# Squared scores read from PSUM, another split of the low parts, and routing candidates written to PSUM

## The chip, the cores and the metric

The kernel runs on one core of one Trainium2 chip. The metric is the device time of one execution in microseconds (us). "The engines" are TensorE (PE in the profile, PEld for its weight loads), VectorE (DVE), ScalarE (ACT), GpSimd (POOL) and SyncE (SP), which issues the DMAs. Each takes its own instructions strictly in the order in which the program lists them, and waits on semaphores of the others.

## What is computed

```python
# u, v: (8, 3136, 256), z: (8, 3136, 64); float32; capacity 128
scores = (1.0 / S) * np.matmul(z, z.transpose(0, 2, 1))
attn = np.maximum(scores, 0.0) ** 2
x = u * np.matmul(attn, v)
s = np.einsum('bsd,d->bs', x, w_gate)
for b in range(B):                       # the 128 tokens of highest s pass through an FFN
    top_idx = np.argpartition(-s[b], capacity)[:capacity]
    xe = x[b, top_idx]
    ye = np.maximum(xe @ w1, 0.0) @ w2
    g = 1.0 / (1.0 + np.exp(-s[b, top_idx]))
    out[b, top_idx] = xe + g[:, None] * ye
```

## The kernel before

**Tiling.** For each of 8 batches the columns of the attention matrix (tokens of the output) are cut into seven chunks: five of 512 and two of 288. The rows come in 24 blocks of 128 and a remainder of 64. A *slot* is one pair of row blocks against one chunk (`slots`, L259): 12 pairs and one single (the remainder) per chunk, 91 slots a batch. The matrix is symmetric, so what lies below the diagonal of whole chunks has been computed before: such an *old* slot fetches its squares from DRAM (`fetch`), a *new* slot computes them. Chunk 0 has new slots alone, chunk 1 has 10 new pairs and 2 old, chunk 2 has 8 and 4, and chunks 5 and 6 have 2 and 10.

**Precision.** Every float32 operand is split in a rounded high part and the low remainder. A new slot takes four score matmuls (`sc`, L314: two row blocks, two halves of Z), an old one none; each pair slot takes 12 matmuls into the two accumulators (`acc`, L391): eight with the high part `hi` of the squares, four with the low part `lo`.

**A new slot's way.** PE writes the scores to `sc` (PSUM; two buffers of two banks each). ACT makes `a` = relu(scale x `sc`) (L317, two buffers) and `hi` = round(`a` squared) (L319). Then `a` is squared in place, by DVE as `a` times `a` (L324) or, when the planner's counters hold DVE for busier than ACT, by ACT (L322). In `low`, DVE transposes `a` in two pieces for the symmetric half (`aT`, L341; SyncE stores it), and `lo` = `a` - `hi` is made by POOL or DVE (L352). `low` of an old slot does only the last step, from `qk`.

**Order.** The program is written out by hand, slot by slot (L1045 on). `mix(k)` emits the 12 accumulation matmuls of slot k and, in the middle of them, the scores of slot k+3; behind it stand the routing steps due in that slot and `low` of slot k+3. A table `busy` of estimated work per engine (`spend`) picks the engine for the squares and for `lo`. At a chunk's end `finish` multiplies both accumulators with `u` on DVE (`ut`, L436), which frees them; there are three accumulator banks, and a chunk takes two.

**Routing.** The 128 best tokens of a batch are found during the next batch, as a search for the threshold in eight rounds of four bits. A round is: PE adds up counts over partitions (`tot`, L556); DVE settles the four bits (`enough`, `mi`, `base`, L561 to L567), makes 15 candidates out of a table of keys in three operations on 98 partitions x 15 numbers (`cand`, `flip`, `key`, L533, L524, L528), compares all scores with them (`ge`, L542) and counts (`cnt`, L550). Rounds stand three slots apart (two in the last batch), so they fall into chunks 0, 1 and 2 of the next batch. The last batch, which has nobody behind it, routes most of its tokens during its own chunks.

Of the kernel before, what the change touches and what calls it, by code (L numbers as in the profile page):

```python
# [10 lines left out]
F32 = mybir.dt.float32  # L11
# [7 lines left out]
P = 128  # L19
# [58 lines left out]
def attention_then_routed_ffn(ctx: ExitStack, tc: tile.TileContext, zt, ut, v, wg, w1, w2, cst, cst16, keys, outs, at, cap):  # L78
# [158 lines left out]
    def prep_v(b, g):  # L237
# [11 lines left out]
        spend(act=0.6, pool=1.5)  # L249
# [53 lines left out]

    def scores(k):
# [12 lines left out]
        nc.scalar.activation(a, ps[:, :n], AF.Relu, scale=SCALE)  # L317
        rows = slice(0, P) if n == 2 else slice(64, P)
        nc.scalar.activation(hi, a, AF.Square)  # L319
        on_act = n == 2 and busy["dve"] > busy["act"]  # L320
        if on_act:
            nc.scalar.activation(a, a, AF.Square)  # L322
        else:
            nc.vector.tensor_tensor(a[rows], a[rows], a[rows], op=ALU.mult)  # L324
        of = w * n
        act, dve = 0.15 + 0.00083 * of, 0.1 + 0.0011 * of
        spend(act=(3 if on_act else 2) * act, dve=0.0 if on_act else dve)
        lows.append((k, a, hi, None))

    def low(k, a, hi, by):  # L330
# [15 lines left out]
        if n == 2:  # L346
            lo = work.tile([P, 2, CH], F32R, name="lo", tag="lo", bufs=LEAD)[:, :, :w]
            on, took = nc.vector, 0.1 + 0.0026 * w
            if busy["pool"] + 0.8 + 0.0034 * w < busy["dve"] + took:
                on, took = nc.gpsimd, 0.65 + 0.0034 * w  # L350
# [3 lines left out]
        else:  # L354
            nc.vector.tensor_tensor(hi[rows], a[rows], hi[rows].bitcast(F32), op=ALU.subtract)
            spend(dve=0.1 + 0.0013 * w)
# [72 lines left out]
    def finish(b, c):  # L429
# [5 lines left out]
        for h in range(NK):  # L435
            nc.vector.tensor_tensor(xT[:, h, :w], acc[b, c][h], xT[:, h, :w], op=ALU.mult)  # L436
        spend(dve=0.1 + 0.0026 * w)
# [6 lines left out]
        def turn(h):  # L444
# [8 lines left out]
            if scored:  # L453
# [6 lines left out]
                spend(pool=0.65 + 0.0034 * w)  # L460
# [40 lines left out]
    def route(b):  # L501
# [18 lines left out]
        def to_float(k):  # L520

            n = k.shape[1]
            m = moe.tile([TP, n], I32, name="flip", tag=f"flip{n}")[:R]
            nc.vector.tensor_scalar(  # L524
                m, k, 31, 0x7FFFFFFF, op0=ALU.arith_shift_right, op1=ALU.bitwise_and
            )
            f = moe.tile([TP, n], I32, name="key", tag=f"key{n}")[:R]
            nc.vector.tensor_tensor(f, k, m, op=ALU.bitwise_xor)  # L528
            return f.bitcast(F32)

        def tries(rd):
            k = moe.tile([TP, NS], I32, name="cand", tag="cand")[:R]
            nc.vector.tensor_scalar(  # L533
                k, consts["keys"][:R, rd * NS : (rd + 1) * NS], st["base"], None, op0=ALU.bitwise_xor
            )
            st["f"] = to_float(k)
            spend(dve=0.6)

        def count():
# [12 lines left out]
            spend(dve=1.3)  # L552
# [5 lines left out]
        def settle(rd):  # L558
# [570 lines left out]
```

## Time and profile before

| what | value |
|---|---|
| runs | median 2385.51 us of 3 (2382.0 to 2386.51) |
| the profiled execution | 2383.7 us, span 2381.9 us |
| PE busy | 2177.3 us (91% of the span) |
| DVE busy | 1866.6 us (78%) |
| ACT busy | 1283.3 us (54%) |
| POOL busy | 1218.1 us (51%) |
| DMA queue of SyncE | 397.66 MB, 67.5% of 16 engines' span |
| granted TensorE clock | 0.970 |

The span runs from the first to the last instruction. Busy time counts an engine's instructions, also while one of them stands and waits inside for something that it shares with another engine; time between instructions is idle time, and the profile names what ended it. Where a row gives `min/median/max`, these are durations in ns of one instruction of that kind. Batches 1 to 6 repeat nearly exactly; batch 0 has a start and no routing beside it, batch 7 has the late routing and the end.

### The profile page before, as it was taken

What the parts mean: (1) busy time and instruction counts of PE and PEld (TensorE: products, weight loads), DVE (VectorE), ACT (ScalarE), POOL (GpSimd) and SP (SyncE); (2) the same over time, 40 slices, a digit from 0 to 9 for tenths busy, and PEclk for the clock granted to TensorE, in tenths of its full rate; (3) what the DMA queues carried; (4) which work ended last, traced back from release to release, by engine and by line L of the source; (5) the groups of instructions that cost most, each with busy time, mean ns of one, the idle gap of its engine ahead of it and who ended that gap; (6) DMA issues with size and microseconds to landing.
All of it is one profiled execution on the core that took longest, in us unless ns stands there. A gap on an engine that the chain in (4) does not pass through costs nothing. (4 is left out here: it accounts for less than half of the span.)

```text
span 2381.9 us, 30970 instructions
## 1 busy us (share of the span) xinstructions
PE 2177.3 (91%) x10593; PEld 1796.8 (75%) x10593; DVE 1866.6 (78%) x2409; ACT 1283.3 (54%) x1502; POOL 1218.1 (51%) x573
## 2 busy tenths in 40 slices
PE   7999988999889998899988999889998899899887
PEld 4778966789667886678866788668886688777676
DVE  6767688876898778986789767897688877887876
ACT  5665555546555465554655546545474555655432
POOL 5664264543556445554555536465374553645532
PEclk8999999999999999999999999999998999999989
DMA  4798855698457974589745996468964588546762
GB/s 132 186 266 185 178 145 135 165 218 196 142 135 183 212 196 130 144 198 205 190 130 146 203 218 187 118 151 188 231 183 119 156 173 197 161 131 142 166 142 65
DMA packets 505758, 401.73 MB, mean 169 GB/s; under 512 B 125952, under 2 KB 416768, under 8 KB 501888
## 3 DMA queue, kind: packets, MB, share of 16 engines
q1 hardware_dynamic: 504832, 397.66, 67.5%
q0 software_dynamic: 768, 2.10, 0.3%
q8 instruction: 83, 1.36, 0.3%
q14 instruction: 75, 0.61, 0.1%
HBM read 225.07 MB, written 162.00 MB: 163 GB/s over the span
## 5 line engine op out<-in xcount | busy, mean ns | idle before, releaser
L391 PE MATMUL acc<-hi,V 128*128 128x512 f32 (+1 forms) x5376 | 1267.6, 374 | 63.0 <-DVE ut L436 57.0
L391 PEld LDWEIGHTS acc<-hi,V 128*128 128x128 f32 x5376 | 952.8, 192 | 296.1 <-DVE ut L436 70.3
L352 POOL TENSOR_TENSOR lo<-a,hi 128x1024 fp32r<-128x1024 f32 (+1 forms) x276 | 661.8, 2401 | 813.6 <-DVE a L324 365.0
L317 ACT ACTIVATE a<-sc 128x1024 f32<-128x1024 f32 (+3 forms) x408 | 379.6, 931 | 638.8 <-PE sc L314 399.0
L391 PE MATMUL acc<-lo,V 128*128 128x512 f32 (+1 forms) x2688 | 679.2, 369 | 25.8 <-POOL lo L352 20.8
L391 PEld LDWEIGHTS acc<-lo,V 128*128 128x128 f32 x2688 | 481.3, 191 | 126.6 <-POOL lo L352 34.9
L324 DVE TENSOR_TENSOR a<-a 128x1024 f32<-128x1024 f32 (+3 forms) x270 | 380.1, 1408 | 238.7 <-ACT hi L319 228.5
L319 ACT ACTIVATE hi<-a 128x1024 fp32r<-128x1024 f32 (+3 forms) x408 | 394.0, 966 | 80.1 <-PE acc L391 64.4
L352 DVE TENSOR_TENSOR lo<-qk,hi 128x576 fp32r<-128x576 f32 (+1 forms) x257 | 351.8, 1377 | 71.2 <-ACT hi L300 62.9
L341 DVE STREAM_TRANSPOSE aT<-a 128x512 f32<-128x512 f32 (+1 forms) x520 | 338.8, 686 | 73.5 <-ACT a L322 51.2
L300 ACT CAST hi<-qk 128x1024 fp32r<-128x1024 f32 (+1 forms) x320 | 273.5, 860 | 211.6 <-PE acc L391 171.7
L314 PE MATMUL sc<-Z,ZL 128*128 128x512 f32 (+1 forms) x760 | 295.7, 390 | 10.1 <-DVE ZL L114 10.1
L314 PE MATMUL sc<-Z,ZH 128*128 128x512 f32 (+1 forms) x760 | 294.8, 389 | 7.3 <-ACT ZH L113 4.3
L114 POOL TENSOR_TENSOR V<-vst,V 128x512 fp32r<-128x512 f32 x96 | 171.7, 1792 | 69.5 <-ACT V L113 69.4
L454 POOL TENSOR_TENSOR ut<-x,w_run 128x1024 f32<-128x1024 f32 (+1 forms) x52 | 135.2, 2600 | 130.4 <-DVE x L445 119.0
L352 POOL TENSOR_TENSOR lo<-qk,hi 128x1024 fp32r<-128x1024 f32 (+1 forms) x63 | 140.7, 2235 | 73.8 <-ACT hi L300 54.1
L314 PEld LDWEIGHTS sc<-Z,ZL 128*128 128x128 f32 x760 | 145.3, 191 | 43.5 <-DVE ZL L114 11.8
L314 PEld LDWEIGHTS sc<-Z,ZH 128*128 128x128 f32 x760 | 145.1, 191 | 36.3 <-ACT ZH L113 5.2
L322 ACT ACTIVATE a<-a 128x1024 f32<-128x1024 f32 (+1 forms) x138 | 137.0, 993 | 4.4
L352 DVE TENSOR_TENSOR lo<-a,hi 128x1024 fp32r<-128x1024 f32 (+1 forms) x76 | 106.2, 1398 | 27.0 <-ACT a L322 25.5
L533 DVE TENSOR_SCALAR cand<-k_sb,base 98x15 int32<-98x15 int32 (+1 forms) x64 | 103.5, 1617 | 2.2
L114 POOL TENSOR_TENSOR ZL<-zst,ZH 128x512 fp32r<-128x512 f32 (+2 forms) x49 | 72.3, 1476 | 33.1 <-ACT ZH L113 33.1
(131 smaller groups left out, 1150.0 us busy)
## 6 DMA issues: line engine op xcount, KB each, us to landing
squares<-aT SPq DMA_DIRECT2D x240, 512.0 KB
qk<-squares SPq DMA_DIRECT2D x320, 256.0 KB
qk<-squares SPq DMA_DIRECT2D x320, 144.0 KB
vst<-in_v SPq DMA_DIRECT2D x96, 256.0 KB
ut<-in_ut SPq DMA_DIRECT2D x40, 512.0 KB
out<-x SPq DMA_DIRECT2D x160, 128.0 KB
zst<-in_zt SPq DMA_DIRECT2D x72, 128.0 KB
wh<-w1h_there SPq DMA_DIRECT2D x6, 1024.0 KB
```

Of the source, the lines that this page charges most:

```text
L114: (lo_on or nc.vector.tensor_tensor)(lo, src, hi.bitcast(F32), op=ALU.subtract)
L300: nc.scalar.copy(by(hi), src)
L314: nc.tensor.matmul(ps[:, q], z[:, j * P : (j + 1) * P], mov, start=start, stop=not start)
L317: nc.scalar.activation(a, ps[:, :n], AF.Relu, scale=SCALE)
L319: nc.scalar.activation(hi, a, AF.Square)
L322: nc.scalar.activation(a, a, AF.Square)
L324: nc.vector.tensor_tensor(a[rows], a[rows], a[rows], op=ALU.mult)
L341: nc.vector.transpose(to, a[rows, q].rearrange("p (t m a) -> p t m a", t=GT, a=Q))
L352: on.tensor_tensor(by(lo), a, by(hi).bitcast(F32), op=ALU.subtract)
L391: nc.tensor.matmul(ac[h], w, mov, start=first and h not in started, stop=stop)
L454: nc.gpsimd.tensor_tensor(wx, runs, consts["wg_run"].rearrange("p (o r) -> p o r", o=1).broadcast_to([P, NB, RUN]), op=ALU.mult,)
L533: nc.vector.tensor_scalar(k, consts["keys"][:R, rd * NS : (rd + 1) * NS], st["base"], None, op0=ALU.bitwise_xor)
```

## The change

Four things, all of them in `scores`, `low`, `finish` and `route`:

1. `a` = relu(`sc`) without the scale; the square is made as `sc` times `a`, with `sc` read from PSUM by DVE. The scale moves into `finish`, which becomes a `scalar_tensor_tensor`.
2. ACT takes the third square only when it is behind DVE by the planner's counters with that work included.
3. The planner tries POOL first for `lo`, with other costs, and gives it to DVE only when POOL is behind by 1.2 us more.
4. Candidates: the keys of round 0 are flipped on the host, the base is kept flipped from round 0 on, and a round's 15 candidates come from one operation, which writes them into columns 128 to 142 of the PSUM bank that holds the totals; `ge` reads them there.

By kind of instruction: squares of pairs on DVE go from 214 to 303 (207 to 273 of them 1024 wide), on ACT from 138 to 49. `lo` on DVE goes from 333 to 260, on POOL from 339 to 412. Sixty-four `cand`, 64 `flip` and 64 `key` become 56 one-step candidates and 8 copies; three one-number operations a batch move from the last round to the first.

```diff
     keys = [(steps << sh) & 0xFFFFFFFF for sh in range(32 - BITS, -1, -BITS)]
+    keys[0] ^= 1 << 31
+    keys[0] = np.where(keys[0] >> 31, keys[0] ^ 0x7FFFFFFF, keys[0])
...
+        act, dve = 0.13 + 0.0008 * w * n, 0.15 + 0.00104 * w * n
+        turned = 0.16 + 0.00118 * w * n if turns(k) else 0.0
-        nc.scalar.activation(a, ps[:, :n], AF.Relu, scale=SCALE)
+        nc.scalar.activation(a, ps[:, :n], AF.Relu)
         nc.scalar.activation(hi, a, AF.Square)
-        on_act = n == 2 and busy["dve"] > busy["act"]
-        if on_act:
+        if n == 2 and busy["act"] + 3 * act < busy["dve"] + dve + turned:
             nc.scalar.activation(a, a, AF.Square)
         else:
-            nc.vector.tensor_tensor(a[rows], a[rows], a[rows], op=ALU.mult)
+            nc.vector.tensor_tensor(a[rows], ps[rows, :n], a[rows], op=ALU.mult)
...
-            on, took = nc.vector, 0.1 + 0.0026 * w
-            if busy["pool"] + 0.8 + 0.0034 * w < busy["dve"] + took:
-                on, took = nc.gpsimd, 0.65 + 0.0034 * w
+            on, took = nc.gpsimd, 0.1 + 0.0042 * w
+            dve = 0.05 + 0.002 * w
+            if busy["pool"] + took > busy["dve"] + dve + (1.2 if busy["pool"] > 0 else 0.0):
+                on, took = nc.vector, dve
...
-            nc.vector.tensor_tensor(xT[:, h, :w], acc[b, c][h], xT[:, h, :w], op=ALU.mult)
+            nc.vector.scalar_tensor_tensor(
+                xT[:, h, :w], acc[b, c][h], SCALE * SCALE, xT[:, h, :w], op0=ALU.mult, op1=ALU.mult
+            )
...
         def tries(rd):
-            k = moe.tile([TP, NS], I32, name="cand", tag="cand")[:R]
-            nc.vector.tensor_scalar(
-                k, consts["keys"][:R, rd * NS : (rd + 1) * NS], st["base"], None, op0=ALU.bitwise_xor
-            )
-            st["f"] = to_float(k)
+            f = st["ps"][:R, 128 : 128 + NS]
+            k = consts["keys"][:R, rd * NS : (rd + 1) * NS]
+            if rd == 0:
+                nc.vector.tensor_copy(f, k.bitcast(F32))
+            else:
+                nc.vector.tensor_scalar(f.bitcast(I32), k, st["base"], None, op0=ALU.bitwise_xor)
+            st["f"] = f
...
+            if rd == 0:
...
+                nc.vector.tensor_scalar(
+                    k, mi, 32 - BITS, INT_MIN, op0=ALU.logical_shift_left, op1=ALU.bitwise_xor
+                )
...
+                nc.vector.tensor_scalar(
+                    flip, k, 31, 0x7FFFFFFF, op0=ALU.arith_shift_right, op1=ALU.bitwise_and
+                )
+                nc.vector.tensor_tensor(base, k, flip, op=ALU.bitwise_xor)
```

What it moves, at two places. DVE's queue where batch 3 goes from chunk 0 to chunk 1, from the second round's settling up to `finish` (`ut` are the two products that free the accumulators). Before:

```order
L324 TENSOR_TENSOR a<-a 128x1024 x2
L561 TENSOR_SCALAR enough,m<-tot 98x15
L565 CAST mi<-m 98x1
L567 TENSOR_SCALAR base<-mi,base 98x1
L533 TENSOR_SCALAR cand<-k_sb,base 98x15
L524 TENSOR_SCALAR flip<-cand 98x15
L528 TENSOR_TENSOR key<-cand,flip 98x15
L542 TENSOR_TENSOR ge<-G,key 98x480
L550 TENSOR_REDUCE cnt<-ge 98x15
L436 TENSOR_TENSOR ut<-acc,ut 128x512 x2
```

DVE's queue at the same place, as changed (the candidates are now `tot`, in the totals' bank):

```order
L332 TENSOR_TENSOR a<-sc,a 128x1024 x2
L563 TENSOR_SCALAR enough,m<-tot 98x15
L567 CAST mi<-m 98x1
L571 TENSOR_SCALAR place<-mi 98x1
L575 TENSOR_SCALAR flip<-place 98x1
L578 TENSOR_TENSOR base<-place,flip 98x1
L537 TENSOR_SCALAR tot<-k_sb,base 98x15
L544 TENSOR_TENSOR ge<-G,tot 98x480
L552 TENSOR_REDUCE cnt<-ge 98x15
L444 SCALAR_TENSOR_TENSOR ut<-acc,ut 128x512 x2
```

The order is the same; the three 15-wide operations ahead of `ge` are one, and in this one round of a batch the base takes three one-number operations in place of one.

PE's queue early in batch 0, one slot's matmuls with what they wait for (the first score matmul of a slot waits until its PSUM buffer is free). Before:

```order
L391 MATMUL acc<-hi,V 128x512 [waits Activation_49]
L391 MATMUL acc<-hi,V 128x512 x7
L314 MATMUL sc<-Z,ZH 128x512 [waits Activation_49]
L314 MATMUL sc<-Z,ZL 128x512
L314 MATMUL sc<-Z,ZH 128x512
L314 MATMUL sc<-Z,ZL 128x512
L391 MATMUL acc<-lo,V 128x512 [waits Pool_49]
```

PE's queue at the same place, as changed:

```order
L399 MATMUL acc<-hi,V 128x512 [waits Activation_49]
L399 MATMUL acc<-hi,V 128x512 x7
L320 MATMUL sc<-Z,ZH 128x512 [waits DVE_49]
L320 MATMUL sc<-Z,ZL 128x512
L320 MATMUL sc<-Z,ZH 128x512
L320 MATMUL sc<-Z,ZL 128x512
L399 MATMUL acc<-lo,V 128x512 [waits Pool_49]
```

The matmuls stand as they stood; the score buffer is now released by DVE's product in place of ACT's relu.

More of the change, by code (lines that the diff above doesn't have):

```diff
@@ L248, in prep_v @@
             V[b, 2 * g + q] = t[:, :, :, q * P : (q + 1) * P]
-        spend(act=0.6, pool=1.5)
+        spend(act=0.6, pool=1.3)
     slots = []
@@ L302, in old_scores, with turns @@
         lows.append((k, src, hi, by))
+    def turns(k):
+        b, c, js, _ = slots[k]
+        return c < WHOLE and js[0] * P >= CHUNKS[c][0] + CH
     def scores(k):
@@ L316, in scores @@
         hi = work.tile([P, 2, CH], F32R, name="hi", tag="hi2", bufs=LEAD)[:, :n, :w]
-        nc.scalar.activation(a, ps[:, :n], AF.Relu, scale=SCALE)
-        rows = slice(0, P) if n == 2 else slice(64, P)
+        act, dve = 0.13 + 0.0008 * w * n, 0.15 + 0.00104 * w * n
+        turned = 0.16 + 0.00118 * w * n if turns(k) else 0.0
+        nc.scalar.activation(a, ps[:, :n], AF.Relu)
         nc.scalar.activation(hi, a, AF.Square)
-        on_act = n == 2 and busy["dve"] > busy["act"]
-        if on_act:
+        if n == 2 and busy["act"] + 3 * act < busy["dve"] + dve + turned:
             nc.scalar.activation(a, a, AF.Square)
+            spend(act=3 * act)
         else:
[L324 to L327, printed above, removed]
+            rows = slice(0, P) if n == 2 else slice(64, P)
+            nc.vector.tensor_tensor(a[rows], ps[rows, :n], a[rows], op=ALU.mult)
+            spend(act=2 * act, dve=dve)
         lows.append((k, a, hi, None))
@@ L336, in low @@
         rows = slice(0, P) if n == 2 else slice(64, P)
-        if c < WHOLE and js[0] * P >= c0 + w:
+        if turns(k):
             t = work.tile([P, 2, CH], F32, name="aT", tag="aT", bufs=2)
@@ L341, in low @@
                 nc.vector.transpose(to, a[rows, q].rearrange("p (t m a) -> p t m a", t=GT, a=Q))
-                spend(dve=0.1 + 0.0013 * w)
+                spend(dve=0.08 + 0.00118 * w)
             at = js[0] * P - c0 - w
@@ L355, in low @@
             nc.vector.tensor_tensor(hi[rows], a[rows], hi[rows].bitcast(F32), op=ALU.subtract)
-            spend(dve=0.1 + 0.0013 * w)
+            spend(dve=0.05 + 0.001 * w)
         parts[k] = (hi, lo)
@@ L435, in finish @@
         for h in range(NK):
-            nc.vector.tensor_tensor(xT[:, h, :w], acc[b, c][h], xT[:, h, :w], op=ALU.mult)
-        spend(dve=0.1 + 0.0026 * w)
+            nc.vector.scalar_tensor_tensor(
+                xT[:, h, :w], acc[b, c][h], SCALE * SCALE, xT[:, h, :w], op0=ALU.mult, op1=ALU.mult
+            )
+        spend(dve=0.1 + 0.0023 * w)
         del acc[b, c]
@@ L459, in turn @@
                 )
-                spend(pool=0.65 + 0.0034 * w)
+                spend(pool=0.1 + 0.0042 * w)
         def add():
@@ L515, in start @@
             nc.vector.tensor_copy(G, st["ps"][:R, :NT])
-            st["base"] = moe.tile([TP, 1], I32, name="base", tag="base", bufs=2)[:R]
-            nc.vector.memset(st["base"], INT_MIN)
             tries(0)
[L520 to L525, printed above, removed]
-            )
-            f = moe.tile([TP, n], I32, name="key", tag=f"key{n}")[:R]
-            nc.vector.tensor_tensor(f, k, m, op=ALU.bitwise_xor)
-            return f.bitcast(F32)
-        def tries(rd):
-            k = moe.tile([TP, NS], I32, name="cand", tag="cand")[:R]
-            nc.vector.tensor_scalar(
-                k, consts["keys"][:R, rd * NS : (rd + 1) * NS], st["base"], None, op0=ALU.bitwise_xor
-            )
-            st["f"] = to_float(k)
-            spend(dve=0.6)
+        def tries(rd):
+            f = st["ps"][:R, 128 : 128 + NS]
[5 more added lines that the diff above has]
+            st["f"] = f
+            spend(dve=0.2)
         def count():
@@ L551, in count @@
             st["n"] = n
-            spend(dve=1.3)
+            spend(dve=1.4)
         def total():
@@ L566, in settle @@
             base = moe.tile([TP, 1], I32, name="base", tag="base", bufs=2)[:R]
-            nc.vector.tensor_scalar(
-                base, mi, 32 - BITS * (rd + 1), st["base"], op0=ALU.logical_shift_left, op1=ALU.bitwise_xor
-            )
+            if rd == 0:
+                k = moe.tile([TP, 1], I32, name="place", tag="place")[:R]
+                nc.vector.tensor_scalar(
+                    k, mi, 32 - BITS, INT_MIN, op0=ALU.logical_shift_left, op1=ALU.bitwise_xor
+                )
+                flip = moe.tile([TP, 1], I32, name="flip", tag="flip")[:R]
+                nc.vector.tensor_scalar(
+                    flip, k, 31, 0x7FFFFFFF, op0=ALU.arith_shift_right, op1=ALU.bitwise_and
+                )
+                nc.vector.tensor_tensor(base, k, flip, op=ALU.bitwise_xor)
+            else:
+                nc.vector.tensor_scalar(
+                    base, mi, 32 - BITS * (rd + 1), st["base"], op0=ALU.logical_shift_left, op1=ALU.bitwise_xor
+                )
             st["base"] = base
-            spend(dve=0.9)
+            spend(dve=0.6)
         def masks():
-            t = to_float(st["base"])
+            t = st["base"].bitcast(F32)
             mk = moe.tile([TP, 2 * NT], BF16, name="mk", tag="mk")[:R]
```

## The prediction

> **What bounds the kernel now.** I read the page first, then the busy time by stretch, then the waits, then the order of time around the longest wait.
>
> ```profile
> span 2381.9 us, 30970 instructions
> PE 2177.3 (91%) x10593; PEld 1796.8 (75%) x10593; DVE 1866.6 (78%) x2409; ACT 1283.3 (54%) x1502; POOL 1218.1 (51%) x573
> ```
>
> PE leads with 91%, so over the whole span only what PE spends waiting can be won. Where it waits is a question of stage. The next rows are busy time by stretch: chunks 1 and 2 of batch 0, which has no routing beside it, then chunks 0, 1 and 2 of batch 3, beside which batch 2 is routed (each stretch runs from a chunk's first accumulation matmul to the next chunk's).
>
> ```profile
> core 0: us, PE busy (x) PEld busy (x) DVE busy (x) ACT busy (x) POOL busy (x), PEclk, DMA share, GB/s
> 81.90:128.30 46.40, 44.40 (x192) 35.42 (x191) 32.71 (x35) 29.94 (x32) 31.59 (x15) 1.00 0.62 177
> 128.30:170.80 42.50, 40.98 (x179) 33.31 (x178) 28.05 (x31) 27.71 (x30) 29.99 (x14) 1.00 0.91 285
> 876.60:924.50 47.90, 45.46 (x198) 36.55 (x197) 43.78 (x48) 33.13 (x38) 33.57 (x17) 1.00 0.62 180
> 924.50:986.30 61.80, 49.12 (x195) 38.12 (x194) 53.69 (x73) 29.87 (x30) 29.72 (x13) 0.92 0.43 120
> 986.30:1034.20 47.90, 42.72 (x186) 33.59 (x185) 41.62 (x62) 25.62 (x26) 26.31 (x12) 1.00 0.62 151
> ```
>
> Chunk 1 is the same attention work in both batches, yet takes 46.4 us in batch 0 and 61.8 in batch 3. DVE is busy 32.7 us in the one and 53.7 in the other: more than the 46.4 that the chunk would need, so DVE bounds this stretch and PE waits, its granted clock down to 0.92. Chunk 2 shows the same in little (42.5 and 47.9). Now the waits of PE, over the span:
>
> ```profile
> PE acc L391 <- DVE ut L436: 57.0, 19, 6.4
> PE tot L556 <- DVE cnt L550: 56.1, 22, 6.4
> ```
>
> Both are waits for DVE: for the products that free the accumulators, and for a round's counts. The longest at the start of chunk 1 of batch 3, in order of time:
>
> ```profile
> 925.62 2.60 DVE L324 TENSOR_TENSOR a<-a 128x1024 f32<-128x1024 f32 x1 [0.99 <-ACT hi L319]
> ...
> 928.79 1.96 DVE L533 TENSOR_SCALAR cand<-k_sb,base 98x15 int32<-98x15 int32 x1
> 930.78 2.25 DVE L524 TENSOR_SCALAR flip<-cand 98x15 int32<-98x15 int32 x1
> 933.06 0.17 DVE L528 TENSOR_TENSOR key<-cand,flip 98x15 int32<-98x15 int32 x1
> 933.27 0.66 DVE L542 TENSOR_TENSOR ge<-G,key 98x480 bf16<-98x480 f32 x1
> 933.96 0.66 DVE L550 TENSOR_REDUCE cnt<-ge 98x15 bf16<-98x480 bf16 x1
> 934.53 1.28 DVE L436 TENSOR_TENSOR ut<-acc,ut 128x512 f32<-128x512 f32 x2
> ```
>
> POOL's rows at the same time, and PE's:
>
> ```profile
> 928.37 2.35 POOL L352 TENSOR_TENSOR lo<-a,hi 128x1024 fp32r<-128x1024 f32 x1 [1.22 <-DVE enough L561]
> 930.67 2.32 POOL L352 TENSOR_TENSOR lo<-qk,hi 128x1024 fp32r<-128x1024 f32 x1
> ```
>
> ```profile
> 935.27 2.07 PE L391 MATMUL acc<-hi,V 128*128 128x512 f32 x4 [6.40 <-DVE ut L436]
> ```
>
> `cand` works on 15 numbers and takes 1.96 us: it ends at 930.75, just as POOL's 2.35 us end (930.72). `flip` ends at 933.03, as POOL's next does (932.99). `key`, with POOL idle, takes 0.17. So some DVE operations stand still until POOL's running one is over. The durations by line say which:
>
> ```profile
> L324 DVE TENSOR_TENSOR a<-a x270: 455/1226/3350, 12.3 to 2345.5; 128x1024 f32<-128x1024 f32 x111, 64x288 f32<-64x288 f32 x15, 64x512 f32<-64x512 f32 x9
> L533 DVE TENSOR_SCALAR cand<-k_sb,base x64: 225/2005/2457, 335.3 to 2275.5; 98x15 int32<-98x15 int32 x56, 48x15 int32<-48x15 int32 x8
> L436 DVE TENSOR_TENSOR ut<-acc,ut x112: 442/679/684, 84.4 to 2351.9; 128x512 f32<-128x512 f32 x80, 128x288 f32<-128x288 f32 x32
> ```
>
> The product of `a` with itself, both operands in SBUF, reaches 3.35 us against a median of 1.23, and `cand` is nearly always slow; `ut`, with one operand in PSUM, never spreads (684 at most, 679 in the middle), wherever POOL stands.
>
> **The change part by part.** *The square from PSUM.* Its price before is the 1507 ns mean of chunk 1 in the rows below. After, the form is that of `ut`, one operand in PSUM: 442 ns at 288 elements and 679 at 512 is 1.06 ns an element, so 1.22 us at 1024, without spread. No row is a reason for less; the upper end is the 1.51 of today, if reading `sc` were to block as well. I take 1.22, `ut` being the same form. The Trainium skill, Trace Analysis, "Optimizing Scalar/DVE Operations", speaks against this edit: it gives DVE some 60 ns of access overhead on SBUF and 125 on PSUM. By that a product would cost 65 ns more, an estimate of 23 us of DVE time over 359 products. The trace does not show it: `ut` from PSUM takes 679 ns where the 64x512 product from SBUF takes 0.69 us (the row at 921.36 below).
>
> *Candidates.* The groups of DVE in chunk 1 of batch 3 (count, then busy us and mean ns):
>
> ```profile
> L324 DVE TENSOR_TENSOR a<-a 128x1024 f32<-128x1024 f32 (+1 forms) x7 | 10.5, 1507 | 3.3 <-ACT hi L319 3.2
> L533 DVE TENSOR_SCALAR cand<-k_sb,base 98x15 int32<-98x15 int32 x5 | 7.4, 1486 | 0.2
> L524 DVE TENSOR_SCALAR flip<-cand 98x15 int32<-98x15 int32 x4 | 7.1, 1763 | 0.1
> L528 DVE TENSOR_TENSOR key<-cand,flip 98x15 int32<-98x15 int32 x4 | 5.0, 1242 | 0.1
> L542 DVE TENSOR_TENSOR ge<-G,key 98x480 bf16<-98x480 f32 x4 | 4.4, 1096 | 0.0
> ```
>
> Three operations, 7.4 + 7.1 + 5.0 = 19.5 us, become five of a kind that no row shows (SBUF to PSUM). Nearest are the unblocked `key` and `cand` (0.17 us, and 225 ns at the least); the far end is `cand` as it is, 1.5 us. I take 0.22, by `cand` without POOL: 1.1 us. `ge` has one operand in PSUM then, and I take it as unblocked too, 4 x 0.66 = 2.6 for 4.4 (at worst no gain). The three one-number steps that move into round 0 stood in the last round; no sum.
>
> *The planner.* In chunk 1 the squares on DVE go from 6 pairs to 8, `lo` on DVE from 2 to 1. Squares: 8 x 1.22 + 0.69 = 10.4 for 10.5. `lo`: 1.2 less.
>
> DVE in chunk 1: 53.7 - 19.5 + 1.1 - 1.8 - 0.1 - 1.2 = 32.2 us. That is what batch 0 has there (32.7), in 46.4 us. So chunk 1 stops being bound by DVE, and I price it by batch 0's row, plus what is left of the routing chain at its start. There, from 928.15 (settling) to 934.53 DVE took 6.4 us; now settling with its one-number steps some 1.2, candidates 0.22, `ge` 0.66, `cnt` 0.66: 2.7. The product before it shrinks by 2.60 - 1.22 = 1.4. So `ut` comes 5.1 us earlier, and of PE's 6.4 us 1.3 stay; with what POOL's `lo` may add I keep 1.6. **Chunk 1: 46.4 + 1.6 = 48.0, that is 13.8 less. Chunk 2:** batch 0's 42.5 and 1.0 for a round that is still late: 43.5, **4.4 less.**
>
> *The new wait.* A slot's first score matmul now waits until DVE has multiplied the slot two before it, not until ACT has read it; behind it on PE stand the `lo` matmuls and everything else. Where it bites first is the end of chunk 0:
>
> ```profile
> 914.07 1.81 DVE L324 TENSOR_TENSOR a<-a 128x1024 f32<-128x1024 f32 x1 [1.04 <-ACT hi L319]
> ...
> 921.36 0.69 DVE L324 TENSOR_TENSOR a<-a 64x512 f32<-64x512 f32 x1
> ```
>
> ```profile
> 918.13 0.39 PE L314 MATMUL sc<-Z,ZH 128*128 128x512 f32 x1
> ...
> 923.52 1.17 PE L391 MATMUL acc<-hi,Vr 128*128 128x512 f32 x4 [1.96 <-DVE hi L355]
> ```
>
> The scores at 918.13 would need the product that ended at 922.05: 3.9 us late. As changed, DVE goes on from 914.07: product 1.22, `G` and keys 0.22 each, two transposes (some 0.7 each, an estimate by the 0.69 that DVE needs for 512 elements) 1.4, `ge` and `cnt` 0.66 each, product 0.69: done at 919.1, 1.0 late. In return the 1.96 us that PE waits for the single slot's `hi` at 923.52 go, as all that stands before it on DVE ends 3 us earlier. **Chunk 0: 1.0 less.** Bounds: 3.9 us of new wait (2 us worse than now), or none.
>
> *The rest.* In chunks 3 to 6 batches gain nothing: DVE has room there. Moving 73 `lo` to POOL costs
>
> ```profile
> L352 POOL TENSOR_TENSOR lo<-a,hi 128x1024 fp32r<-128x1024 f32 x262 | 641.4, 2451 | 717.1 <-DVE a L324 365.0 <-DVE enough L561 157.7 <-PE acc L391 60.6
> L352 DVE TENSOR_TENSOR lo<-a,hi 128x1024 fp32r<-128x1024 f32 x58 | 86.3, 1488 | 18.8 <-ACT a L322 18.1
> ```
>
> up to 1.0 us more each, hidden by three slots of lead; POOL in chunk 0 goes from 33.6 to 33.6 + 2 x 2.45 = 38.5 of 47 us. The longer `finish` operation is hidden the same way. Batch 7 from chunk 0 to 5:
>
> ```profile
> PE tot L556 <- DVE cnt L550: 18.3, 4, 6.4
> ```
>
> Each of the four waits shrinks by what the candidates save, at most 4.3 us (4.5 by the three means of chunk 1, less 0.22), and none by more than itself: I take 15, and 2 at the chunk ends, **17 less** (between 8 and the whole 18, and as much again if the low clock behind such waits goes too). Batch 0 has no routing: nothing.
>
> **Sum.** Six batches x (13.8 + 4.4 + 1.0) = 115, and 17: 132 us. The profiled execution took 2383.7 us (span 2381.9), 1.8 below the median of the runs: 2383.7 - 132 = 2251.7, and on the median's footing 2253.5.
>
> **The rivals.** *All of it:* DVE's queue stays short enough that batches 1 to 6 run at batch 0's pace (6 x (15.4 + 5.4 + 2) = 137) and batch 7 loses all of its 18.3 and as much again in low clock: 174, or **2212**. For it: chunk 1's DVE load comes out at batch 0's. Against: the chain at the start of chunk 1 is still there.
>
> *POOL takes DVE's place.* POOL's 412 `lo` come in bursts behind other POOL work, each is slower, and it blocks DVE's remaining 260. If each of the 73 moved shows as 1.0 us at PE: 132 - 73 = 59 less, **2326**. For it: POOL in chunk 0 comes to 82%. Against: chunk 1 of batch 0 ran with 9 of 12 `lo` on POOL in 46.4 us. The Trainium skill has this rule: Trace Analysis, "Optimizing Scalar/DVE Operations", says that moving work between GpSimd and DVE might not help, as they share a port. The rows of `cand` and `flip` agree that one waits for the other.
>
> *Half:* the waits are not for the blocked operations but for DVE's queue as such, and products that ACT gave back fill it: only the 56.1 us of waits for counts go, and the time is **2329**.
>
> *Slower:* the score buffers bind. Scores, relu, `hi` and product of a slot now hold a buffer in one chain, and with two buffers PE waits in each new slot of chunks 0 and 1, where all or nearly all slots are new. That decides as soon as the product ends later than two slots after its scores; at 918.13 today's queue would miss by 3.9. If the 22 pairs of both chunks in 8 batches lose 1 us each, 176 us stand against 132: **2430**. Against: today's queue misses by 3.9 only behind `cand`, `flip` and blocked products, and DVE's load falls in chunk 0 too, from 43.8 by two `lo` (3.0) and a round's candidates (4.3) and rises by three more squares (11 x 1.22 - 8 x 1.51 = 1.3): 37.8 of 47 us.
>
> That the candidates are still blocked when written to PSUM is a rival too: 64 x 1.3 = 83 us of DVE, about half of the gain; it is counted with *half*.
>
> **How the numbers follow.** Forecast 0.58 (own range 2225 to 2280), all of it 0.15, POOL 0.10, half 0.12, slower 0.05. From 2200 to 2328 the range holds the forecast, most of *all of it* and somewhat over half of *POOL* and *half*, whose times lie at its upper edge: 8 in 10. A measurement of this kernel tells about 0.2%, 5 us, from no change. Of *half* and *POOL* I give 0.03 to ends within those 5 us, so: faster 0.92, same 0.03, slower 0.05.
>
> **What would show it.** Right: chunk 1 of batch 3 near 48 us with DVE busy near 32 and clock 1.00; squares at 1.22 us with no spread, candidates near 0.2; waits for counts below 15 us and for `ut` below 20. Wrong: PE's score matmuls waiting for DVE's product by more than 30 us in sum, or `lo` of POOL at the head of PE's waits, or candidates near 1.5 us.

## The result, and the profile after

| | median us | runs | ratio to before (95% interval) |
|---|---|---|---|
| before, in the same comparison | 2386.01 | 4 | |
| changed | 2229.12 (2226.57 to 2232.8) | 4 | 0.9339 (0.9308 to 0.9369) |

The changed kernel is 157 us faster where 132 were forecast. Its page begins as follows (busy time and share of the span by engine).

```profile
span 2225.4 us, 30970 instructions
PE 2141.4 (96%) x10593; PEld 1779.0 (80%) x10593; DVE 1574.0 (71%) x2289; ACT 1203.5 (54%) x1413; POOL 1315.2 (59%) x646
```

DVE lost 293 us of busy time, POOL took on 97, and PE went from 91% to 96%. The same stretches as in the prediction: chunks 1 and 2 of batch 0, then chunks 0, 1, 2 and 6 of batch 3.

```profile
core 0: us, PE busy (x) PEld busy (x) DVE busy (x) ACT busy (x) POOL busy (x), PEclk, DMA share, GB/s
75.83:121.44 45.61, 45.01 (x191) 36.02 (x190) 29.73 (x35) 26.91 (x30) 34.85 (x17) 0.97 0.62 177
121.44:164.19 42.75, 41.00 (x180) 33.34 (x178) 28.40 (x33) 25.03 (x28) 31.62 (x15) 1.00 0.96 285
833.43:878.45 45.02, 45.02 (x198) 36.57 (x197) 34.82 (x47) 31.10 (x36) 35.29 (x20) 1.00 0.65 192
878.45:927.52 49.07, 46.13 (x195) 36.79 (x194) 35.61 (x69) 26.87 (x27) 29.84 (x14) 0.97 0.55 149
927.52:969.99 42.47, 42.45 (x186) 33.60 (x185) 33.59 (x55) 24.67 (x25) 22.55 (x10) 1.00 0.72 175
1073.95:1101.94 27.99, 27.37 (x200) 26.48 (x199) 14.11 (x19) 16.60 (x26) 18.17 (x13) 1.00 0.90 219
```

Chunk 1 of batch 3 went from 61.80 us to 49.07 and its DVE work from 53.69 to 35.61; chunk 0 is now PE alone (45.02 busy of 45.02), chunk 2 next to that. What is left of PE's waits:

```profile
PE acc L399 <- DVE ut L444: 23.2, 8, 4.4
PE acc L399 <- DVE lo L360: 11.3, 7, 3.3
PE acc L399 <- POOL lo L360: 8.9, 12, 1.8
PE tot L558 <- DVE cnt L552: 1.9, 2, 1.6
PE sc L320 <- DVE a L332: 0.5, 1, 0.5
```

The waits for counts are gone (56.1 to 1.9), those for `ut` more than halved (57.0 to 23.2), and the new wait of the scores for DVE's product hardly exists (0.5). The wait for low parts made by DVE has grown. Before it was

```profile
PE acc L391 <- DVE lo L352: 4.9, 6, 1.0
```

The durations behind this (min/median/max in ns):

```profile
L332 DVE TENSOR_TENSOR a<-sc,a x359: 460/1224/1228, 12.1 to 2187.4; 128x1024 f32<-128x1024 f32 x136, 64x512 f32<-64x512 f32 x21, 128x576 f32<-128x576 f32 x15, 64x288 f32<-64x288 f32 x8
L537 DVE TENSOR_SCALAR tot<-k_sb,base x56: 227/236/240, 338.8 to 2118.6; 98x15 int32<-98x15 int32 x49, 48x15 int32<-48x15 int32 x7
L544 DVE TENSOR_TENSOR ge<-G,tot x56: 602/614/655, 339.1 to 2120.3; 98x480 bf16<-98x480 f32 x49, 48x480 bf16<-48x480 f32 x7
L578 DVE TENSOR_TENSOR base<-place,flip x8: 1850/1854/1910, 336.9 to 2075.9; 98x1 int32<-98x1 int32 x7, 48x1 int32<-48x1 int32 x1
```

Three of the four lost their spread: whatever has one operand or its result in PSUM runs its own time (square 1.22 us, at most 1.23; candidates 0.24, comparison 0.61). The eight comparisons of round 0 read the bank of `gate` and are not in this row. The fourth, `base` from `place` and `flip`, works on one number, has both operands in SBUF, and takes 1.85 us each time. It stands at the one place where that hurts, at the start of chunk 1. DVE's rows there, then POOL's and PE's:

```profile
879.65 0.15 DVE L575 TENSOR_SCALAR flip<-place 98x1 int32<-98x1 int32 x1
879.84 1.87 DVE L578 TENSOR_TENSOR base<-place,flip 98x1 int32<-98x1 int32 x1
881.74 0.24 DVE L537 TENSOR_SCALAR tot<-k_sb,base 98x15 int32<-98x15 int32 x1
882.02 0.66 DVE L544 TENSOR_TENSOR ge<-G,tot 98x480 bf16<-98x480 f32 x1
882.71 0.66 DVE L552 TENSOR_REDUCE cnt<-ge 98x15 bf16<-98x480 bf16 x1
883.28 1.28 DVE L444 SCALAR_TENSOR_TENSOR ut<-acc,ut 128x512 f32<-128x512 f32 x2
```

```profile
876.94 4.75 POOL L360 TENSOR_TENSOR lo<-a,hi 128x1024 fp32r<-128x1024 f32 x2 [5.02 <-DVE a L332]
```

```profile
878.45 1.08 PE L399 MATMUL acc<-hi,V 128*128 128x512 f32 x4
884.01 2.08 PE L399 MATMUL acc<-hi,V 128*128 128x512 f32 x4 [2.94 <-DVE ut L444]
```

`base` ends at 881.71, as POOL's second low part ends (881.69). PE waits 2.94 us for the first `ut`, where it waited 6.40. The four matmuls behind the wait take 2.08 us, the same four ahead of it 1.08.

That the slow operations wait for POOL is no chance of one place. All 8 `base` of this trace end 11 to 17 ns after a POOL operation ends. In the kernel before, 51 of 64 `cand` are slow and all 51 end within 0.1 us of the end of a POOL operation; none of the 13 quick ones lies wholly inside one. As changed, 52 of the 56 candidates lie wholly inside a POOL operation and take at most 240 ns.

Where the time came from, batches 1 to 6 together: the first number of each row is the sum of the six stretches. Before, chunks 0, 1, 2 and 6:

```profile
sum 287.56, PE 272.89 PEld 219.28 DVE 262.61 ACT 198.96 POOL 201.43; mean PE 45.48 PEld 36.55 DVE 43.77 ACT 33.16 POOL 33.57
sum 370.99, PE 296.40 PEld 229.37 DVE 322.51 ACT 178.99 POOL 178.13; mean PE 49.40 PEld 38.23 DVE 53.75 ACT 29.83 POOL 29.69
sum 288.44, PE 257.90 PEld 202.65 DVE 249.80 ACT 153.73 POOL 158.16; mean PE 42.98 PEld 33.77 DVE 41.63 ACT 25.62 POOL 26.36
sum 167.29, PE 161.11 PEld 155.47 DVE 113.79 ACT 101.08 POOL 72.92; mean PE 26.85 PEld 25.91 DVE 18.96 ACT 16.85 POOL 12.15
```

As changed, the same chunks in the same order:

```profile
sum 270.11, PE 270.11 PEld 219.42 DVE 208.87 ACT 186.53 POOL 213.68; mean PE 45.02 PEld 36.57 DVE 34.81 ACT 31.09 POOL 35.61
sum 291.68, PE 273.40 PEld 219.25 DVE 213.78 ACT 161.21 POOL 177.59; mean PE 45.57 PEld 36.54 DVE 35.63 ACT 26.87 POOL 29.60
sum 254.69, PE 254.57 PEld 201.68 DVE 201.22 ACT 148.02 POOL 135.09; mean PE 42.43 PEld 33.61 DVE 33.54 ACT 24.67 POOL 22.52
sum 178.68, PE 165.38 PEld 158.71 DVE 95.67 ACT 99.28 POOL 107.75; mean PE 27.56 PEld 26.45 DVE 15.94 ACT 16.55 POOL 17.96
```

Chunk 0 gave 17.5 us, chunk 1 79.3, chunk 2 33.8; chunks 3 to 5 nothing in sum; chunk 6 took 11.4 back. The chunk 6 of batch 3 shown above is not one of those that lost; that of batch 2 went from 28.00 us to 32.19. There, DVE's row, POOL's and PE's:

```profile
817.29 3.87 DVE L360 TENSOR_TENSOR lo<-qk,hi 128x576 fp32r<-128x576 f32 x1 [0.33 <-DMA qk<-squares]
```

```profile
819.12 1.41 POOL L360 TENSOR_TENSOR lo<-qk,hi 128x576 fp32r<-128x576 f32 x1
```

```profile
821.21 0.80 PE L399 MATMUL acc<-lo,V 128*128 128x288 f32 x4 [2.14 <-DVE lo L360]
```

A low part of this size takes DVE 743 ns at the least; this one takes 3.87 us beside POOL's operations, and PE waits for it. Of the 11.3 us that PE waits for DVE's low parts, 10.3 lie in chunk 6 of batches 1 to 6; before, all of the 4.9 lay there.

The four chunks make 119 us of the 156.5 by which the span fell. The rest is batch 0 (5) and batch 7, whose first six chunks went so:

```profile
2031.30:2311.70 280.40, 253.13 (x1160) 202.31 (x1159) 222.33 (x357) 145.25 (x160) 139.18 (x64) 0.95 0.61 151
```

```profile
1906.50:2153.90 247.40, 240.85 (x1159) 193.79 (x1158) 193.61 (x332) 133.20 (x148) 142.41 (x67) 1.00 0.69 171
```

33 us less, with the granted clock up from 0.95 to 1.00: PE's idle time fell by 20.7 us and its busy time by 12.3; the end behind them took 1.3 us more.

### The profile page after: what moved, and what is told of

The parts are those of the page before. It is cut to its first block, busy times and chain, and to the rows that moved or that the text cites. A ratio compares the mean times of both kernels' runs of the same rounds, so it can differ in the third digit from the quotient of the medians.

```text
span 2225.4 us, 30970 instructions
## 1 busy us (share of the span) xinstructions
PE 2141.4 (96%) x10593; PEld 1779.0 (80%) x10593; DVE 1574.0 (71%) x2289; ACT 1203.5 (54%) x1413; POOL 1315.2 (59%) x646
## 5 line engine op out<-in xcount | busy, mean ns | idle before, releaser
L399 PE MATMUL acc<-hi,V 128*128 128x512 f32 (+1 forms) x5376 | 1245.1, 370 | 26.8 <-DVE ut L444 23.2
L360 POOL TENSOR_TENSOR lo<-a,hi 128x1024 fp32r<-128x1024 f32 (+1 forms) x321 | 779.5, 2430 | 658.1 <-DVE a L332 370.9
L399 PEld LDWEIGHTS acc<-hi,V 128*128 128x128 f32 x5376 | 940.0, 190 | 197.3 <-DVE ut L444 32.9
L399 PE MATMUL acc<-lo,V 128*128 128x512 f32 (+1 forms) x2688 | 672.7, 367 | 20.2 <-DVE lo L360 11.3
L332 DVE TENSOR_TENSOR a<-sc,a 128x1024 f32<-128x1024 f32 (+2 forms) x359 | 391.7, 1091 | 422.2 <-ACT hi L326 352.8
L360 DVE TENSOR_TENSOR lo<-qk,hi 128x1024 fp32r<-128x1024 f32 (+1 forms) x229 | 347.6, 1523 | 79.6 <-ACT hi L302 69.2
L360 POOL TENSOR_TENSOR lo<-qk,hi 128x576 fp32r<-128x576 f32 (+1 forms) x91 | 163.2, 1796 | 127.1 <-ACT hi L302 114.5
L116 POOL TENSOR_TENSOR V<-vst,V 128x512 fp32r<-128x512 f32 x96 | 139.7, 1459 | 25.2 <-ACT V L115 25.0
L115 ACT CAST V<-vst 128x512 fp32r<-128x512 f32 x96 | 58.4, 608 | 49.7 <-DMA vst<-in_v 49.6
L455 DVE STREAM_TRANSPOSE x<-ut 128x512 f32<-128x512 f32 (+1 forms) x112 | 68.1, 622 | 0.0
L444 DVE SCALAR_TENSOR_TENSOR ut<-acc,ut 128x512 f32<-128x512 f32 (+1 forms) x112 | 64.3, 615 | 1.0 <-PE sc L320 0.5
```

The costliest lines, as they stand in the source:

```text
L116: (lo_on or nc.vector.tensor_tensor)(lo, src, hi.bitcast(F32), op=ALU.subtract)
L332: nc.vector.tensor_tensor(a[rows], ps[rows, :n], a[rows], op=ALU.mult)
L360: on.tensor_tensor(by(lo), a, by(hi).bitcast(F32), op=ALU.subtract)
L399: nc.tensor.matmul(ac[h], w, mov, start=first and h not in started, stop=stop)
L444: nc.vector.scalar_tensor_tensor(xT[:, h, :w], acc[b, c][h], SCALE * SCALE, xT[:, h, :w], op0=ALU.mult, op1=ALU.mult)
L455: nc.vector.transpose(x[:, :, h, :], xT[:, h, :w].rearrange("p (f q) -> p f q", q=Q))
```

## The experiments

My theory was that DVE bounds chunks 0 to 2 while the batch before is routed, because its SBUF-only operations stand behind POOL's, and that the routing's are the costlier ones. The rivals: the squares are the larger part; POOL first is itself the gain; fewer operations count, not their place. All ratios are to the kernel before, on the same chip as the run.

| kernel | median us | ratio (95% interval) |
|---|---|---|
| changed | 2229.12 | 0.9339 (0.9308 to 0.9369) |
| routing_alone | 2262.79 | 0.9493 (0.9473 to 0.9513) |
| psum_squares_alone | 2343.96 | 0.9827 (0.9804 to 0.9850) |
| planner_alone | 2447.94 | 1.0284 (1.0250 to 1.0317) |
| no_planner | 2222.73 | 0.9321 (0.9303 to 0.9338) |
| candidates_in_sbuf | 2277.45 | 0.9561 (0.9536 to 0.9585) |
| squares_from_sbuf | 2307.91 | 0.9681 (0.9664 to 0.9698) |
| old_lo_rule | 2217.19 | 0.9303 (0.9277 to 0.9328) |
| place_in_psum | 2205.59 | 0.9247 (0.9222 to 0.9273) |
| no_round_at_end | 2232.45 | 0.9365 (0.9341 to 0.9388) |
| both | 2230.79 | 0.9346 (0.9319 to 0.9372) |
| place_old_lo | 2198.43 | 0.9211 (0.9196 to 0.9227) |
| no_planner_place | 2200.59 | 0.9229 (0.9214 to 0.9245) |

**routing_alone.** The kernel before, with the hunks of `route` and of the keys.

```diff
-            st["f"] = to_float(k)
+            f = st["ps"][:R, 128 : 128 + NS]
+                nc.vector.tensor_scalar(f.bitcast(I32), k, st["base"], None, op0=ALU.bitwise_xor)
```

> The kernel before with the candidates alone changed (one operation a round, written to PSUM); squares, finish and planner's rules as before. My theory, that DVE's blocked operations of the routing bound chunks 1 and 2 of batches 1 to 6: most of the gain, 105 to 135 of the 157 us (2251 to 2281 us), chunk 1 of batch 3 near 50 us with DVE near 34. Rival, that the squares read from SBUF were the larger part: at most 60 us (2326 or more), with chunk 1 still above 55 us.

Measured: 121 us less than before, inside the range and 77% of what the whole change gave. (The planner counts the new routing as lighter work for DVE, and so gives it 16 low parts more.) Chunk 1 of batch 3:

```profile
889.05:941.00 51.95, 46.18 (x195) 36.75 (x194) 39.00 (x70) 29.82 (x30) 26.88 (x12) 0.97 0.53 145
```

DVE's 53.69 us there fell to 39.00, more than the 34 expected. The squares are not the reason, as they took 10.5 us of both: the stretch now holds a fifth comparison and count, one low part more, and `base` from two SBUF operands with 1.82 us. The chunk is no longer bound by DVE. The rival that made the squares the larger part falls.

**psum_squares_alone.** The kernel before, with the square from PSUM and the scale in `finish`.

```diff
-            nc.vector.tensor_tensor(a[rows], a[rows], a[rows], op=ALU.mult)
+            nc.vector.tensor_tensor(a[rows], ps[rows, :n], a[rows], op=ALU.mult)
```

> The kernel before with the squares alone changed (scores times relu out of PSUM, scale in finish); routing and planner as before, so the same 214 squares on DVE. My theory: each square loses its blocked time, 207 x 0.36 = 75 us of DVE, of which little lies in the stretch that DVE bounds; 2345 to 2380 us, with DVE still above 50 us in chunk 1 of batch 3, and PE's score matmuls waiting for DVE there now and then. Rival (squares the larger part): 2290 or less. Rival (score buffers held longer by a late DVE cost more than is won): 2390 or more.

Measured: 2343.96, 40 us less than before: 1 us under my range and far from both rivals. The squares lose all spread, and here the new wait is to be seen, since DVE is still late:

```profile
L324 DVE TENSOR_TENSOR a<-sc,a x270: 460/1224/1227, 11.1 to 2309.4; 128x1024 f32<-128x1024 f32 x111, 64x288 f32<-64x288 f32 x15, 64x512 f32<-64x512 f32 x9
```

```profile
PE sc L314 <- DVE a L324: 14.0, 15, 1.6
```

14.0 us, against 0.5 in the changed kernel: the score buffers bind only while DVE's queue is long.

**planner_alone.** The changed kernel's rules, with squares from SBUF and routing as before.

```diff
+            on, took = nc.gpsimd, 0.1 + 0.0042 * w
+            if busy["pool"] + took > busy["dve"] + dve + (1.2 if busy["pool"] > 0 else 0.0):
+                on, took = nc.vector, dve
```

> The changed kernel's rules for who squares and who makes the low parts, with squares out of SBUF and routing as before. My theory: 89 more squares on DVE and 92 more low parts on POOL, both against each other: DVE in chunk 1 above 54 us; slower than before, 2395 to 2450. Rival (POOL first is itself a gain): 2370 or less.

Measured: 64 us slower than before, inside the range; DVE in chunk 1 of batch 3 is busy for 55.49 us. Chunk 0 of batch 3 is bound by DVE outright, 51.24 us busy of 52.10:

```profile
897.00:949.10 52.10, 46.35 (x199) 36.22 (x198) 51.24 (x49) 30.34 (x35) 40.56 (x19) 1.00 0.57 166
```

That the new rules are a gain by themselves is refuted. This run moves two things, squares from ACT to DVE and low parts from DVE to POOL, and cannot tell which of them loses. The Trainium skill, Perfetto Trace Analysis, "Optimizing Scalar/DVE Operations", says that moving work between GpSimd and DVE might not help because they share a port. The run nearest to that question is old_lo_rule below, with the squares read from PSUM: it gives 71 low parts back to DVE and is no slower than the changed kernel (2217.19 us against 2229.12).

**no_planner.** The two parts that gained, with the planner of before (the edit, against the changed kernel, in part).

```diff
-        if n == 2 and busy["act"] + 3 * act < busy["dve"] + dve + turned:
+        on_act = n == 2 and busy["dve"] > busy["act"]
+        if on_act:
```

> The squares from PSUM and the new candidates together, with the planner's rules of before (who squares, who makes the low parts): the changed kernel without its parts 2 and 3. Alone the two gave 121 and 41 us, the planner's part alone lost 64. My theory: the planner's part is worth next to nothing once the squares are read from PSUM, and its low parts on POOL cost chunk 6 about 2 us a batch: 2212 to 2232 us. Rival, that the gain beyond the two parts came of the new rules (157 against 121 + 41 - 64): 2250 or more.

Measured: 163 us less than before, close to the sum of the two alone (121 + 40). The interval overlaps that of the changed kernel: the new rules neither add nor cost what this can tell. Chunk 6 of batches 1 to 6 takes 167.70 us in place of 178.68. The rules cost 64 us in planner_alone, and 45 between routing_alone and squares_from_sbuf (2262.79 and 2307.91), which both have the new candidates and squares from SBUF; so their loss goes with squares that stand behind POOL's operations.

**squares_from_sbuf.** The changed kernel with its squares from SBUF.

```diff
-            nc.vector.tensor_tensor(a[rows], ps[rows, :n], a[rows], op=ALU.mult)
+            nc.vector.tensor_tensor(a[rows], a[rows], a[rows], op=ALU.mult)
```

> The changed kernel with its squares read from SBUF again (a times a), all else as changed: 303 squares of pairs on DVE stand behind POOL's operations again. My theory: each takes 0.4 to 0.5 us longer, 130 us of DVE, most of it in chunks 0 and 1 where DVE has 10 to 13 us of room a batch; 2255 to 2290 us. Rival, that the source of the squares does not matter once the routing is light: within 10 us of 2229.

Measured: 2307.91, 79 us above the changed kernel, more than my theory allowed and far from the rival. So the place of the squares is worth 40 us under the old rules (with the old routing and, routing_alone against no_planner, with the new) and 79 under the new ones, which put more squares on DVE and more work on POOL against them. Sums over batches 1 to 6, chunks 0 and 1:

```profile
sum 295.67, PE 277.05 PEld 217.27 DVE 288.84 ACT 180.97 POOL 243.42; mean PE 46.18 PEld 36.21 DVE 48.14 ACT 30.16 POOL 40.57
sum 318.80, PE 283.74 PEld 224.80 DVE 234.42 ACT 166.75 POOL 188.93; mean PE 47.29 PEld 37.47 DVE 39.07 ACT 27.79 POOL 31.49
```

Chunk 0 takes 25.6 us more and chunk 1 27.1; DVE in chunk 0 rises from 34.8 us to 48.1 a batch, above PE's 46.2.

**candidates_in_sbuf.** One operation as in the change, but into SBUF.

```diff
-            f = st["ps"][:R, 128 : 128 + NS]
+            f = moe.tile([TP, NS], F32, name="cand", tag="cand")[:R]
```

> The changed kernel with the one candidate operation writing to SBUF in place of PSUM, so that the number of operations stays and the place alone is undone. My theory, that the place counts because SBUF-only operations stand behind POOL's: candidates 1.5 to 2 us each in place of 0.24 and the comparison up to 1 us in place of 0.62, wait of PE for the accumulators at the start of chunk 1 longer by 2 to 3 us a batch; 2240 to 2262 us. Rival, that three operations becoming one is all: within 6 us of the changed kernel's 2229.

Measured: 2277.45, 48 us above the changed kernel. The place counts, and more than I had put on it, because the comparison with it falls behind POOL nearly always (median 1.70 us, not 0.61), and with it every round. Chunk 1 of batches 1 to 6 takes 22.6 us more than in the changed kernel and chunk 2 16.9. What the two operations fewer are worth by themselves was not separated. The durations:

```profile
L537 DVE TENSOR_SCALAR cand<-k_sb,base x56: 225/1931/2349, 339.1 to 2162.3; 98x15 int32<-98x15 int32 x49, 48x15 int32<-48x15 int32 x7
L544 DVE TENSOR_TENSOR ge<-G,cand x64: 606/1699/2781, 328.1 to 2164.0; 98x480 bf16<-98x480 f32 x56, 48x480 bf16<-48x480 f32 x8
```

**place_in_psum.** The one-number step that feeds `base` goes to PSUM.

```diff
-                k = moe.tile([TP, 1], I32, name="place", tag="place")[:R]
+                k = st["ps"][:R, 160:161].bitcast(I32)
```

> The changed kernel with the one-number step of round 0 (place) written to PSUM, so that the step after it (base) has one operand in PSUM. In the changed kernel that step takes 1.86 us and stands right ahead of finish's products, for which PE waits 3 us at the start of chunk 1. My theory: it takes 0.2 us, PE's wait there loses 1.6 us in each of batches 1 to 6 and the low clock behind it: 10 to 20 us less than the changed kernel's 2229 (2209 to 2219). Rival, that finish's products wait for something else: within 4 us of 2229.

Measured: 2205.59, ratio 0.9247 (0.9222 to 0.9273), below the changed kernel's interval. Eight one-number operations were worth some 23 us, a little more than expected; in the traces chunk 1 of batches 1 to 6 gives 16.3 of them (291.68 to 275.37), and where the rest comes from is not shown. `base` now takes its own time, and chunk 1 of batch 3 runs in 45.90 us at full clock (49.07 at 0.97):

```profile
L578 DVE TENSOR_TENSOR base<-tot,flip x8: 149/157/159, 340.5 to 2060.1; 98x1 int32<-98x1 int32 x7, 48x1 int32<-48x1 int32 x1
```

```profile
871.60:917.50 45.90, 44.51 (x195) 35.71 (x194) 34.02 (x69) 26.87 (x27) 29.93 (x14) 1.00 0.58 160
```

**no_round_at_end** and **both.** No routing task in the last pair slot of chunk 0, batches 1 to 6; alone, and with `place` in PSUM.

```diff
-            if far and far[0] and rested <= k and (busy["dve"] < 9 if late else not tasks):
+            if far and far[0] and rested <= k and not (c == 0 and 0 < b < B - 1 and k % SLOTS == SLOTS - 2) and (
+                busy["dve"] < 9 if late else not tasks
+            ):
```

> The changed kernel with no routing task in the last pair slot of chunk 0 in batches 1 to 6, so that the second round's steps stand behind finish's products and all later rounds a slot or three later. My theory, that this round's chain is all that holds up the products: PE's 3.2 us wait and the 2 us of low clock behind it go in six batches, 18 to 30 us less than 2229 (2199 to 2211), less what the later rounds cost in chunk 2. Rival, that DVE is late there anyway: within 6 us of 2229.

> The two edits together (place in PSUM, and no routing task in the last pair slot of chunk 0). If both act through the same wait, as my theory has it, the second adds little: within 4 us of the faster of the two alone. If they act apart, their gains add.

Measured: 2232.45 and 2230.79, no gain; both expectations failed. The first lies where its rival put it, but not for the rival's reason, since PE's wait at the start of chunk 1 does go. Chunks 1, 2 and 6 of batches 1 to 6 in no_round_at_end:

```profile
sum 265.80, PE 265.51 PEld 214.83 DVE 208.01 ACT 167.07 POOL 171.05; mean PE 44.25 PEld 35.81 DVE 34.67 ACT 27.85 POOL 28.51
sum 269.74, PE 256.79 PEld 204.66 DVE 202.82 ACT 147.99 POOL 141.69; mean PE 42.80 PEld 34.11 DVE 33.80 ACT 24.66 POOL 23.61
sum 195.84, PE 171.72 PEld 163.17 DVE 108.53 ACT 99.39 POOL 114.94; mean PE 28.62 PEld 27.20 DVE 18.09 ACT 16.57 POOL 19.16
```

Chunk 1 gains 25.9 us (291.68 to 265.80), as the theory had it, but chunk 2 loses 15.0 (254.69 to 269.74) and chunk 6 17.2 (178.68 to 195.84). With the rounds, all that follows them moved later, the FFN's steps among it. For chunk 6 the traces show the next link: in five of the six batches PE waits 2.3 to 3.7 us for `hi` of an old slot, which stands on ACT behind a piece of V whose load has not landed (over the span PE waits 16.0 us for this `hi`, 1.5 in the changed kernel). In batch 3 the FFN's weights are issued at 1077.02, right ahead of that load, and at 1068.61, ten us ahead of it, in the changed kernel. That the weights hold the load up is not shown; no run tried it.

**old_lo_rule.** The changed kernel with the old rule for low parts.

```diff
-            on, took = nc.gpsimd, 0.1 + 0.0042 * w
+            on, took = nc.vector, 0.1 + 0.0026 * w
+            if busy["pool"] + 0.8 + 0.0034 * w < busy["dve"] + took:
+                on, took = nc.gpsimd, 0.65 + 0.0034 * w
```

> The changed kernel with the old rule and costs for who makes the low parts (DVE 331, POOL 341, about as before). My theory: POOL first was worth little by itself: within 12 us of 2229, chunk 6 shorter by about 1 to 2 us a batch (less wait for low parts that DVE makes behind POOL), chunk 1 a little longer. Rival, that POOL first carries a good part of the gain: 2250 or more.

Measured: 2217.19, inside the range; by the intervals not told apart from the changed kernel. (Through the planner's counters 19 squares of pairs go back to ACT with the rule.) Chunk 6 of batches 1 to 6 is back to what it was before (167.29), and chunk 1 takes 0.8 us more in all:

```profile
sum 167.83, PE 162.06 PEld 155.67 DVE 114.18 ACT 98.89 POOL 74.62; mean PE 27.01 PEld 25.95 DVE 19.03 ACT 16.48 POOL 12.44
```

**place_old_lo** and **no_planner_place.** The two edits together, and `place` in PSUM on top of no_planner.

> The changed kernel with both edits that gained alone: the one-number step of round 0 in PSUM (24 us) and the old rule for the low parts (12 us). My theory: they act in different chunks (1 and 6) and add: 2188 to 2200 us. Rival, that they act on the same waits: 2203 or more.

> The squares from PSUM and the new candidates, the old planner's rules, and the one-number step of round 0 in PSUM. My theory: 15 to 25 us less than the same kernel without the last, so 2190 to 2212 us, about the same as the changed kernel with the old rule for the low parts alone and that step. Rival, that the rule for who squares matters by itself: over 10 us away from that one.

Measured: 2198.43, ratio 0.9211 (0.9196 to 0.9227), and 2200.59, ratio 0.9229. Place_old_lo beats both kernels of this study: 1.4% less than the changed one (0.9211 / 0.9339). It lies inside my range and below the rival's 2203. The two gains add (alone 0.0092 and 0.0036 of the time before, together 0.0128), as they should from different chunks, and who squares makes no difference that can be told.

## Why the prediction was right, point by point

- **DVE bounds chunks 1 and 2, by operations that stand behind POOL's.** Right, and shown: with the candidates alone 121 us go; with their place alone undone 48 come back, and before the change every slow `cand` ends with an operation of POOL.
- **Prices.** Candidate 0.22 forecast, 0.236 measured; comparison 0.66 and 0.614; square 1.22 and 1.224. The Trainium skill, Perfetto Trace Analysis, "Optimizing Scalar/DVE Operations", gives DVE some 60 ns of access overhead on SBUF and 125 on PSUM. That difference does not show here: the square's median is 1224 ns from PSUM, and 1226 from SBUF before.
- **Chunk 1.** Forecast 13.8 us a batch, measured 79.3 / 6 = 13.2; 49.07 us in batch 3 for a forecast of 48.0. DVE's busy time there came to 35.6 us for 32.2: a fifth comparison and count stand in the stretch, and `base`. The chain at its start was priced at 1.3 to 1.6 us of remaining wait and left 2.94: I took the one-number steps as some 1.2 us in sum, and `base` alone is 1.87. In the last round of the kernel before, the same step had a median of 694 ns, also far above its own time; I had called its move to round 0 no cost. (Two operations moved, not three: the flip and the exclusive or that makes `base`; `place` stands where the old `base` stood.) Two of my signs did not come: `ut` below 20 us (23.2) and a clock of 1.00 there (0.97).
- **Chunk 2.** 4.4 forecast, 33.8 / 6 = 5.6 measured. No round is late there any more.
- **Chunk 0, and the new wait.** 1.0 forecast, 17.5 / 6 = 2.9 measured. The term that failed is "1.0 late" for the scores: I let DVE start from the time that it had before. Its squares no longer stand behind POOL from the chunk's beginning, so it is not late at the end: the scores wait 0.5 us in the whole run, and the 2.45 us that PE stood idle in this chunk of each batch are gone. The mechanism is real: 14.0 us in psum_squares_alone.
- **Chunks 3 to 6 "gain nothing", the 73 low parts "hidden by three slots of lead".** Wrong in chunk 6, by 11.4 us. The slots there are short, and a low part that DVE makes waits for POOL, which has more to do (12.15 us of busy time a batch before, 17.96 as changed). PE's waits for DVE's low parts there went from 4.9 us to 10.3, and with the old rule chunk 6 is 10.9 us shorter again.
- **Batch 7.** 17 forecast, 31.7 measured. The waits went as forecast; the low clock behind them (0.95 to 1.00 over the first six chunks) went too, which the prediction had named as the far bound and not counted. This is the largest mis-sized term. It goes back to the first step, that over the whole span "only what PE spends waiting can be won": PE's busy time fell too, from 2177.3 to 2141.4 us, with the same matmuls.
- **Batch 0.** 0 forecast, 5.4 measured, all of it ahead of chunk 1, which starts at 75.83 us for 81.90. The traces point to the squares: from the first accumulation matmul to chunk 1 the stretch takes 58.6 us before and in routing_alone, with DVE busy for 45 us, and 53.6 in psum_squares_alone, with 36.3. In the four kernels with squares from SBUF it takes 58.6 to 60.2 us, in the ten with squares from PSUM 52.8 to 57.2. "Batch 0 has no routing: nothing" left out that the squares are blocked there as well.
- **Rivals.** POOL does not take DVE's place, except for chunk 6. The score buffers do not bind. "All of it" (2212) was nearer to the measured time than the forecast.
- **The sum.** The mechanism was right and the total is 25 us off. That it is not further off is in part luck: the 11.5 us too little in chunk 0 and the 11.4 us of loss in chunk 6 that was put at nothing cancel.

## What to carry to other kernels

A small DVE operation whose time spreads up to the length of a running POOL operation is not slow but waiting; compare its minimum with its median before counting operations, and give it one operand or its result in PSUM. Price a stall together with the low TensorE clock that follows it, since both went at once here: of the 79.3 us of chunk 1, 56.3 are idle time of PE and 23.0 busy time. A rule that decides which engine takes a piece of work is worth what it is worth only beside the placement of the operands: here the same rules cost 45 to 64 us with squares in SBUF and nothing that can be told with squares in PSUM.

## What the runs showed of the hardware that I had not expected

- One number on 98 partitions waits as long as a thousand: `base` with two operands in SBUF took 1854 ns beside POOL's low parts and 157 ns with one operand in PSUM. One-number operations with a single tensor operand do not wait: in the changed kernel `flip` ran in 0.15 us while POOL was busy (879.65, POOL's row from 876.94 to 881.69), as did all eight of them, and 53 of the 56 later `base` from `mi` lie wholly inside a POOL operation and take at most 215 ns.
- For the candidates a result in PSUM is enough: they read their keys and the base from SBUF and write to PSUM, and never took more than 240 ns; the same operation writing to SBUF had a median of 1931. An operation on two tensors in SBUF with its result alone in PSUM was not tried.
